# Feature order turned, edge columns with the folds, leads and delays per unit, load order and last store of an FNet-plus-FFN kernel

## The chip, the cores and the metric

The kernel runs on one core of a Trainium2 chip. The metric is the device time of one execution in microseconds; of several runs the median is taken. TensorE (PE) multiplies matrices and writes to PSUM. VectorE (DVE) and ScalarE (ACT) do arithmetic on SBUF and PSUM, GpSimd (POOL) on SBUF. SyncE (SP), ACT and POOL issue DMAs, each on a queue of its own. Every engine takes its instructions in the order in which they were written and waits on semaphores of the others.

## The reference

```python
def _attn_ref(x):                      # x: 8 x 3008 x 256
    X = np.fft.fft(x, axis=1)
    X = np.fft.fft(X, axis=2)
    return X.real.astype(np.float32)

def _moe_ref(x, w_in, w_out):          # 24064 x 256, 256 x 2048, 2048 x 256
    h = np.maximum(x @ w_in, 0.0)
    return (h * h @ w_out).astype(np.float32)
```

The real part of a two-dimensional Fourier transform of each of eight batches, and on its 24064 rows a feed-forward layer with squared relu.

## The kernel before, in words

**Folding.** The real part of the transform is symmetric, so a batch is handled by half of its rows and half of its columns. `fold_ops(b)` (L326) adds the two mirrored row halves of a batch on DVE (`u`, L334 and L338), makes their sums and differences (`v`, L346), and from each of these two features by adding or subtracting the mirrored columns (`w`, L352, 127 columns). Column 0 is copied to column 127 of `w` (L358) and column 128 to a separate tile of edges (`ez`, L360, for the first two batches, or `eall`, L362).

**Stage one.** `stage1_ops` (L409) multiplies the features by cosine and sine tables of the sequence transform (matmuls `pf`), ACT copies one parity from PSUM (`as`, L398), and DVE adds and subtracts the two parities into `pt` and `qt`, 1505 columns per batch (L427 to L434). The tables are made at the start by DVE (reduction of the angles, L237 to L249), ACT (sine) and mirror copies scaled by small vectors (`alt`, `nalt`, `sgn` and others, made by POOL, L168 to L182). The transform over the columns is folded into the input weights: `gmat` (L301) multiplies w_in by the matrices `csD` to G1 and G2, and `gneg` makes G3.

**Chunks and units.** The 12040 columns of `pt` and `qt` are cut into 25 chunks: two of 256, then 512, the last of 264. A chunk passes 16 units of 128 hidden features; a pair of such units is one step in the two short chunks, and one unit is a step in the others. A step has a front (first matmuls into PSUM tile `xb`) and, `LAG` = 2 steps later, a back (last matmuls into the same tile). Each unit gives the hidden values of a column and those of its mirror column. A letter in `KINDS` (L491) says how:

- r: three matmuls of the chunk's width, both relus on ACT (L607, L675).
- v: the same three, with the mirror's relu on DVE (L672).
- d: two matmuls. DVE makes an edge product X from `eb` and `gE2` (L634) and T = X − 2·xb (L653); ACT does the first relu (L663), DVE the mirror by a custom add with relu (L664).
- q: like d, but ACT copies −2·xb (L650) and POOL adds X (L651).
- p: like d, with X made by POOL (`edge`, L626). It is in the code, but no unit has it.

Pairs of units are squared by DVE (L687) or, where `SQA` (L492) lists them, by ACT in two halves (L684, L685). The second layer, `mm2_ops` (L513), then multiplies the squared values by w_out (matmuls `po`, 128x256), 16 per output tile; two output tiles share a PSUM tile, ACT copies it to SBUF (L558) and SP stores it in one or two DMAs per output tile (L547). The `po` matmuls of a chunk are spread over the steps of the next one.

**What sets the order.** The order is written out by hand: each step emits its front, half of its `po` matmuls, the back of two steps before, the other half, due mirrors (delay `DLAG`, L619, 1 step for all), copies of finished outputs, ACT's second square halves, the next unit's edge product, squares (3 steps after the back, 1 in the two short chunks), and side work: folds, stage one and tables of later batches, spread between fractions of a batch's time (`FOLD`, `ST1`).

**The start.** DMAs of x(0) go out on SP, POOL (gathers) and ACT (four small rows). ACT loads w_in in four quarters behind the second of eight mirror copies (L714). After the folds of batch 0 POOL loads w_out in four parts and then x(1) (L721). Ten warm matmuls on the cleared tile `ez` (L719) keep TensorE busy before the first real ones.

Of the kernel before, what the change touches and what calls it, by code (L numbers as in the profile page):

```python
# [18 lines left out]
HS = 32.0  # L19
# [5 lines left out]
def kernel(  # L25
# [103 lines left out]
    for s in range(2):  # L129
        gather(0, 1 - s)  # L130
        nc.sync.dma_start(out=x4[0:NP, s, :, :], in_=up(0, s))
    jm = h2p.tile([P, 3, P], F32, name="jm", tag="h2")
    jrow = jm[:, 0]
    nc.gpsimd.iota(jrow, pattern=[[1, P]], base=1, channel_multiplier=0,
# [33 lines left out]
    def alt_vecs():  # L168
        nc.gpsimd.tensor_scalar(out=alt, in0=pidx, scalar1=0.5, scalar2=-0.25, op0=ALU.mult, op1=ALU.add)
        nc.gpsimd.tensor_scalar(out=alt2, in0=alt, scalar1=R23, scalar2=None, op0=ALU.add)  # L170
        nc.gpsimd.tensor_scalar(out=alt2, in0=alt2, scalar1=R23, scalar2=None, op0=ALU.subtract)
        nc.gpsimd.tensor_tensor(alt, alt, alt2, op=ALU.subtract)
        nc.gpsimd.tensor_scalar(out=alt, in0=alt, scalar1=4.0, scalar2=None, op0=ALU.mult)
        nc.gpsimd.tensor_scalar(out=nalt, in0=alt, scalar1=-1.0, scalar2=None, op0=ALU.mult)
        nc.gpsimd.tensor_scalar(out=alt1, in0=top, scalar1=2.0, scalar2=alt[:, 0:1], op0=ALU.mult, op1=ALU.add)
        nc.gpsimd.tensor_scalar(out=nalt1, in0=alt1, scalar1=-1.0, scalar2=None, op0=ALU.mult)

    def sgn_vecs():
        nc.gpsimd.tensor_scalar(out=sgn, in0=pidx, scalar1=P - 1.5, scalar2=None, op0=ALU.is_lt)
        nc.gpsimd.tensor_scalar(out=s3, in0=sgn, scalar1=-2.0, scalar2=None, op0=ALU.mult)  # L180
        nc.gpsimd.tensor_scalar(out=sgn, in0=sgn, scalar1=2.0, scalar2=-1.0, op0=ALU.mult, op1=ALU.add)
        nc.gpsimd.tensor_scalar(out=nsgn, in0=sgn, scalar1=-1.0, scalar2=None, op0=ALU.mult)  # L182
# [9 lines left out]
    def dmats():  # L192
        pv = nc.gpsimd
# [6 lines left out]
        pv.memset(csD[:, 0, 0, P - 1 : P], 1.0)  # L200
        alt_vecs()
# [123 lines left out]

    def fold_ops(b):  # L326
        u = uvp.tile([P, 2, NQ, D], F16, name="u", tag="u")
        vs = {}
# [11 lines left out]
        def half(h, s):  # L340
            qs = slice(h * NQ // 2, (h + 1) * NQ // 2)

            def f():
                if h == 0:
                    vs[s] = uvp.tile([P, NQ, D], F16, name="v", tag="v")
                vt(vs[s][k, qs, :], u[k, 0, qs, :], u[k, 1, qs, :],  # L346
                   op=ALU.subtract if s else ALU.add)
            return f

        def feat(i, q):  # L350
            s = i % 2
            return lambda: vt(w[k, i, q : q + 3, 0 : P - 1], vs[s][k, q : q + 3, 1:P],  # L352
                              vs[s][k, q : q + 3, D - 1 : P : -1],
                              op=ALU.add if i < 2 else ALU.subtract)

        def edges(s):
            def f():
                nc.vector.tensor_copy(w[k, s, :, P - 1], vs[s][k, :, 0])  # L358
                if b in INL:
                    nc.vector.tensor_copy(ez[k, s, :, P - 1], vs[s][k, :, P])  # L360
                else:
                    nc.vector.tensor_copy(eall[k, s, :, b], vs[s][k, :, P])  # L362
            return f

        ops = [f for s in range(2) for f in (pair(s, 0), pair(s, 1), pair0(s))]
        if b + 1 < B:
            ops.append(lambda: load_x(b + 1))
        par = [[half(h, s) for h in range(2)] + [edges(s)]
               + [feat(i, q) for i in (s, 2 + s) for q in (0, 3)] for s in range(2)]
# [39 lines left out]
    def stage1_ops(b, blk, inline_e=False, run=3):  # L409
# [12 lines left out]
        def fin(sn):  # L422
            def f(a, bp):
                hi = P - 1 if sn and not inline_e else P
                lo_, hi_ = halves(blk, PQ[b][sn][0:hi])
                if sn and inline_e:
                    stt(out=lo_, in0=a, scalar=sgn[:, 0:1], in1=bp, op0=ALU.mult, op1=ALU.add)  # L427
                    stt(out=hi_, in0=bp, scalar=nsgn[:, 0:1], in1=a, op0=ALU.mult, op1=ALU.add)
                else:
                    vt(lo_, a, bp, op=ALU.add)  # L430
                    if sn:
                        vt(hi_, a, bp, op=ALU.subtract)
                    else:
                        vt(hi_, bp, a, op=ALU.subtract)  # L434
# [56 lines left out]
    KINDS = ["vrvrrrrrrrrrrrrr"] + ["rrrrvrrvrrrrrrrr"] + ["rvrrvvrrrvrrrrrr"] + ["rrrrrrrqdrrdrrrr"] + ["rdqqrrqrqrrrdrrq"] + ["rrrrddrrqrqrdqqq"] + ["rrrrrrqqqddrrdqd"] + ["rrdrqqdrrdrrqrqr"] + ["rqdddrqrrdrdrrdr"] + ["qddrqrdrrrdqddrr"] + ["drddqrdrrrddqrdr"] + ["qrrdrdddrrdrqrqr"] + ["drrdrqdrrddrdrqr"] + ["rrqdrdqrqqrrrddr"] + ["rrddqdqqrrqqdqqq"] + ["rrrrrrqqqddqrqrd"] + ["qdrdddrdqdrqdqrr"] + ["drdqqqrdqrqdrqqr"] + ["qdqqdqrqqrqdrqrq"] + ["dddrdqrdrqqdrqdq"] + ["dddrdqdrqrqdrddr"] + ["qdqqdqrdqrqdrqqr"] + ["qrqddqrqqrqdrqdr"] + ["qdqqdqvqqrqdqrdr"] + ["rddrdddddrdrdrdd"]  # L491
    SQA = [()] + [(3,)] + [(2, 6)] + [(0, 4, 5)] + [(0, 2, 5, 6)] + [(0, 4, 6)] + [(2, 3, 7)] + [(4, 6)] + [(5, 7)] + [(2, 5, 6)] + [(3, 7)] + [(0, 2, 6)] + [(0, 2, 5, 6)] + [(2, 4, 6)] + [(3,)] + [(1, 4, 6, 7)] + [(1, 2, 6)] + [(1, 4, 6)] * 2 + [(1, 4, 5, 6, 7)] + [(1, 4, 6)] * 3 + [(1, 4, 6, 7)] + [(0, 1, 6)]  # L492
# [20 lines left out]
    def mm2_ops(c):  # L513
# [36 lines left out]
        def store(grp, po):  # L550
# [157 lines left out]
    for h in range(2):  # L708
        for f in rd0[5 * h : 5 * h + 5] + (tr0[5:] if h else tr0[:5]):
            f()  # L710
# [163 lines left out]
```

## Time and profile before

| | |
|---|---|
| time, median of 9 runs | 604.55 us (603.03 to 605.39) |
| the profiled execution | 603.28 us |
| its span, first to last instruction | 601.5 us |
| PE busy | 581.4 us (97%) |
| ACT busy | 541.8 us (90%) |
| DVE busy | 526.7 us (88%) |
| POOL busy | 186.7 us (31%) |
| DMA | 56.25 MB, mean 94 GB/s |
| granted TensorE clock, mean | 0.999 |

Busy time counts stretches in which an instruction of the engine runs; ends of matmuls are modelled and overlap the next one, so the mean of one matmul (272 ns for 256 columns) is longer than the spacing of two. A row of a group has line, engine, operation, output and inputs, shape and count; then busy time and mean; then the idle time before, with what ended it. A row in order of time has start, length, engine, line and operation, with merged repeats as "x2".

### The profile page before, as it was taken

Reading aid. Unit: us, or ns where it says so; the run is one execution under the profiler, and the core shown is the slowest. Engines: PE = TensorE matmul, PEld = TensorE weight load, DVE = VectorE, ACT = ScalarE, POOL = GpSimd, SP = SyncE. Lnnn points to the kernel's source line nnn. Section 1 sums busy time; section 2 is a strip of 40 time slices with the busy share of each in tenths; the row PEclk is TensorE's granted clock in tenths of the full one; section 3 lists DMA queues with packets and bytes.
Section 4 is the critical chain, followed back from the end, with each engine's and each line's share of the span. In section 5 each row is a group of like instructions: output and inputs, shape, how many; then the busy total and the mean of one; then the engine's idle time right before and its main releaser. Section 6 shows DMA issues by size and latency. Waiting matters only on the chain.

```text
span 601.5 us, 12271 instructions
## 1 busy us (share of the span) xinstructions
PE 581.4 (97%) x4561; PEld 437.5 (73%) x4561; DVE 526.7 (88%) x954; ACT 541.8 (90%) x965; POOL 186.7 (31%) x177
## 2 busy tenths in 40 slices
PE   2899999999999999999999999999999999999997
PEld 0576676767777777777877778777787778877786
DVE  7899979998998999998889897989999989889880
ACT  5899899999998898889999989998998999999981
POOL 8502216412352014111113152322552323445300
PEclk9999999999999999999999999999999999999999
DMA  8967599673384225823133112331341422432212
GB/s 255 260 129 177 123 204 225 139 197 50 53 209 91 54 58 103 205 42 44 55 62 44 55 39 60 45 47 50 63 62 36 62 41 58 58 48 55 58 54 71
DMA packets 42337, 56.25 MB, mean 94 GB/s; under 512 B 8158, under 2 KB 37138, under 8 KB 42278
## 3 DMA queue, kind: packets, MB, share of 16 engines
q1 hardware_dynamic: 33878, 29.05, 25.8%
q0 software_dynamic: 7264, 24.31, 16.8%
q10 hardware_dynamic: 1136, 2.12, 1.1%
q8 instruction: 35, 0.57, 0.4%
q14 instruction: 24, 0.20, 0.1%
HBM read 29.02 MB, written 24.64 MB: 89 GB/s over the span
## 4 chain that ended last, share of the span: by engine, by line
PE 84%; ACT 9%; DVE 4%; POOL 1%; issue 1%; ACTq 0%; DVEq 0%; POOLq 0%
PE po L73 50%; PE xb L73 29%; PE pf L73 5%; ACT h L607 2%; ACT h L675 1%; ACT h L684 1%; ACT h L663 1%; ACT h L685 1%; DVE h L664 1%; DVE u L334 1%; POOL x L101 1%; ACT bs L650 0%; DVE v L346 0%; ACT os L558 0%; DVE bs L653 0%
## 5 line engine op out<-in xcount | busy, mean ns | idle before, releaser
L73 PE MATMUL po<-wout,h 128*128 128x256 f16 x3024 | 450.0, 272 | 0.0
L73 PEld LDWEIGHTS <-h 128*128 128x128 f16 x3024 | 286.3, 98 | 109.4 <-issue 0.6
L651 POOL TENSOR_TENSOR bs<-bs,h 128x512 f32<-128x512 f32 x99 | 133.7, 1353 | 311.4 <-ACT bs L650 213.2
L73 PE MATMUL xb<-qt,G 128*128 128x512 f16 (+11 forms) x758 | 211.3, 321 | 1.8 <-ACT h L607 0.9
L664 DVE CUSTOM_DVE_ANT_0 h<-xb,bs 128x512 f16<-128x512 f32 (+1 forms) x217 | 137.5, 642 | 24.2 <-ACT h L663 23.2
L687 DVE TENSOR_TENSOR h<-h 128x2048 f16<-128x2048 f16 (+1 forms) x122 | 149.6, 1229 | 0.4 <-ACT h L675 0.4
L73 PE MATMUL xb<-pt,G 128*128 128x512 f16 (+16 forms) x512 | 146.4, 323 | 1.0 <-DVE pt L434 0.5
L73 PEld LDWEIGHTS <-G 128*128 128x128 f16 x1270 | 121.3, 98 | 25.4 <-issue 4.4
L663 ACT ACTIVATE h<-xb 128x512 f16<-128x512 f32 (+1 forms) x206 | 129.1, 628 | 8.2 <-PE xb L73 6.4
L607 ACT ACTIVATE h<-xb 128x512 f16<-128x512 f32 (+1 forms) x178 | 110.6, 625 | 12.8 <-PE xb L73 12.4
L675 ACT ACTIVATE h<-xb 128x512 f16<-128x512 f32 (+2 forms) x174 | 105.3, 609 | 11.3 <-PE xb L73 9.2
L653 DVE SCALAR_TENSOR_TENSOR bs<-xb,h 128x512 f32<-128x512 f32 (+1 forms) x107 | 70.6, 660 | 17.3 <-PE xb L73 13.5
L634 DVE TENSOR_SCALAR h<-eb,gE 128x512 f16<-128x512 f16 (+1 forms) x206 | 79.6, 394 | 0.7 <-DMA eb<-qt 0.7
L685 ACT ACTIVATE h<-h 128x1024 f16<-128x1024 f16 (+1 forms) x70 | 74.9, 1070 | 0.0
L684 ACT ACTIVATE h<-h 128x1024 f16<-128x1024 f16 (+1 forms) x70 | 73.8, 1055 | 0.0
L558 ACT ACTIVATE os<-po 128x512 f32<-128x512 f32 x94 | 59.1, 629 | 8.7 <-PE po L73 8.6
L650 ACT ACTIVATE bs<-xb 128x512 f32<-128x512 f32 x99 | 63.5, 641 | 3.0 <-PE xb L73 1.4
L334 DVE TENSOR_TENSOR u<-x 127x765 f16<-127x765 f32 x32 | 30.6, 976 | 1.0 <-DMA x<-in_x_dram 1.0
L124 POOL DMA_DIRECT2D x<-in_x_dram x14 | 8.3, 593 | 58.8 <-DVE u L338 58.8
L73 PEld LDWEIGHTS <-w 127*128 127x128 f16 (+1 forms) x192 | 21.8, 117 | 5.6 <-DVE cosT L280 0.6
L101 POOL DMA_INDIRECT x<-in_x_dram,idx x18 | 23.4, 1298 | 5.4 <-issue 4.9
L352 DVE TENSOR_TENSOR w<-v 127x381 f16<-127x381 f16 x64 | 21.3, 357 | 0.0
(103 smaller groups left out, 227.4 us busy)
## 6 DMA issues: line engine op xcount, KB each, us to landing
out_dram<-os SPq DMA_DIRECT2D x157, 128.0 KB
x<-in_x_dram POOLq DMA_DIRECT2D x14, 756.0 KB, 10.9
wst<-in_moe_w_in_dram ACTq DMA_DIRECT2D x4, 512.0 KB
eb<-qt SPq DMA_DIRECT2D x14, 128.0 KB
x<-in_x_dram SPq DMA_DIRECT2D x2, 756.0 KB
wout<-in_moe_w_out_dram POOLq DMA_DIRECT2D x4, 256.0 KB, 7.0
x<-in_x_dram,idx POOLq DMA_INDIRECT x18, 11.2
gE<-G SPq DMA_DIRECT2D x16, 0.2 KB
```

Source lines behind the costliest of these rows:

```text
L73: nc.tensor.matmul(o, l, r, start=start, stop=stop, skip_group_check=True)
L607: act(r_s(c, u), xb, AF.Relu, scale=-1.0)
L634: ts(out=X, in0=ebc[c][:, 0:n], scalar1=gE2[:, u : u + 1], scalar2=None, op0=ALU.mult)
L650: act(T, xb, AF.Copy, bias=0.0, scale=-2.0)
L651: nc.gpsimd.tensor_tensor(T, T, X, op=ALU.add)
L653: stt(out=T, in0=xb, scalar=-2.0, in1=X, op0=ALU.mult, op1=ALU.add)
L663: act(r_s(c, u), xb, AF.Relu, scale=-1.0)
L664: mirrors.append((DLAG[KINDS[c][u]], lambda: relu_d(c, u, lambda o, i: nc.vector._custom_dve(TENSOR_ADD_SAT, out=o[:, 0, :], in0=xb[:, 0, ...
L675: relu_d(c, u, lambda o, i: act(o, xb[:, :, i], AF.Relu, scale=-1.0))
L684: act(h2[:, 0:nf], h2[:, 0:nf], AF.Square)
L685: rest.append(lambda: act(h2[:, nf:], h2[:, nf:], AF.Square))
L687: vt(h2, h2, h2, op=ALU.mult)
```

## The change

1. `KINDS` and `SQA` are rewritten: r 185 → 174, v 9 → 11, d 107 → 105, q 99 → 95, p 0 → 15; pairs squared by ACT 70 → 76.
2. Every d, q or p unit has its own lead for the edge product (`LEAD`, in half steps, 2 mostly) and its own delay of the mirror (`DEFER`, 1 mostly); every pair has its own lag of the square (`SQLAG`, 3 mostly; in chunk 0 the lags are 1, 1, 1, 2).
3. The features come in turned order, with 128 columns: `v` gets two zero columns, and column 0 is added to one of them by the same subtraction, so that the copy to column 127 of `w` is gone. `v` is a constant tile now.
4. At the start `alt_vecs`, `sgn_vecs` and the angles of `csD` go from POOL to DVE, the clear of `ez` from DVE to POOL behind the two gathers. 18 warm matmuls instead of 10. One more table operation stands before the second pair of folds.
5. The first quarter of w_in is issued by ACT behind the first mirror, the other three behind the sixth. POOL loads x(1) before w_out.
6. In stage one of batch 0 the second halves of `pt` and `qt` are put off behind both first halves. The stretches for folds and stage one of batches 0 to 2 are shifted a little.
7. In the last output group all 16 matmuls of the first tile come before those of the second, and each half is copied and stored by itself.

```diff
     for s in range(2):
         gather(0, 1 - s)
         nc.sync.dma_start(out=x4[0:NP, s, :, :], in_=up(0, s))
+    nc.gpsimd.memset(ez, 0.0)
...
-    nc.gpsimd.iota(jrow, pattern=[[1, P]], base=1, channel_multiplier=0,
+    nc.gpsimd.iota(jrow, pattern=[[-1, P]], base=P - 1, channel_multiplier=0,
...
-        nc.gpsimd.tensor_scalar(out=alt, in0=pidx, scalar1=0.5, scalar2=-0.25, op0=ALU.mult, op1=ALU.add)
...
+        ts(out=alt, in0=pidx, scalar1=0.5, scalar2=-0.25, op0=ALU.mult, op1=ALU.add)
...
-        pv = nc.gpsimd
+        pv = nc.vector
...
+    vf = const.tile([P, NQ, D + 2], F16, name="v")
+    nc.gpsimd.memset(vf[:, :, D : D + 2], 0.0)
...
-        def feat(i, q):
-            s = i % 2
-            return lambda: vt(w[k, i, q : q + 3, 0 : P - 1], vs[s][k, q : q + 3, 1:P],
-                              vs[s][k, q : q + 3, D - 1 : P : -1],
+        def feat(i, q, n):
+            return lambda: vt(w[k, i, q : q + n, :], vf[k, q : q + n, P - 1 :: -1],
+                              vf[k, q : q + n, P + 1 : D + 1],
                               op=ALU.add if i < 2 else ALU.subtract)
 
         def edges(s):
-            def f():
-                nc.vector.tensor_copy(w[k, s, :, P - 1], vs[s][k, :, 0])
...
+            e = ez[k, s, :, P - 1] if b in INL else eall[k, s, :, b]
+            return lambda: nc.vector.tensor_copy(e, vf[k, :, P])
...
-                    vt(hi_, bp, a, op=ALU.subtract)
+                        later(lambda: vt(hi_, bp, a, op=ALU.subtract))
...
-            act(os_, po, AF.Copy, bias=0.0, scale=HS * HS)
-            for j, (s, t0, m) in enumerate(grp):
+            js = js or slice(0, len(grp))
+            act(os_[:, js], po[:, js], AF.Copy, bias=0.0, scale=HS * HS)
+            for j, (s, t0, m) in list(enumerate(grp))[js]:
...
+                if fc == NFC - 1 and grp is final:
+                    return lambda o=st["o"]: store(grp, o, slice(j, j + 1))
...
+        final = groups[-1] if c == len(chunks) - 1 else None
         for grp in groups:
-            ops += [one(grp, j, fc) for fcs in (range(NFC - 2 * nf), range(NFC - 2 * nf, NFC))
+            cut = NFC if grp is final else NFC - 2 * nf
+            ops += [one(grp, j, fc) for fcs in (range(cut), range(cut, NFC))
                     for j in range(len(grp)) for fc in fcs]
...
-    DLAG = {'q': 1, 'd': 1, 'p': 1}
...
-    for f in rd1[0:2] + mi0[0:2] + [load_w_in] + mi0[2:] + fe[0:3] + rd1[2:3]:
+    for f in rd1[0:2] + mi0[0:1] + [lambda: load_w_in(0)] + mi0[1:6] + [lambda: load_w_in(1, 2, 3)] + mi0[6:] + fe[0:3] + rd1[2:4]:
         f()
...
-    for _ in range(10):
+    for _ in range(18):
         mm(warm, ez[:, 0, 0, :], ez[:, 0, 0:4, :], True, True)
-    for f in fe[3:6] + [load_w_out] + fe[6:]:
+    for f in fe[3:]:
         f()
+    load_w_out()
...
-    spread(rd1[3:], 0, 5)
-    spread(fo, 8, 9)
+    spread(rd1[4:], 0, 5)
+    spread(fo, 7, 13)
...
-    FOLD = {0: [(1, 0.489, 0.896)], 1: [(2, 0.02, 0.073), (3, 0.261, 0.695), (4, 0.581, 0.851)],
+    FOLD = {0: [(1, 0.467, 0.852)], 1: [(2, 0.068, 0.189), (3, 0.261, 0.695), (4, 0.581, 0.851)],
...
-    ST1 = {0: (0.9, 0.945)}
+    ST1 = {0: (0.855, 0.885)}
...
+    for si, (c, u) in enumerate(steps):
+        if KINDS[c][u] in "qdp":
+            l = int(LEAD[c][u])
+            ahead.setdefault((si - l // 2, l % 2), []).append((c, u))
...
+            if v[1] % 2:
+                squares.setdefault(si + int(SQLAG[v[0]][v[1] // 2]), []).append(v)
```

## The prediction

> **What bounds the kernel now.** I read the page's busy shares first, then the chain that ended last, then the costliest groups.
>
> ```profile
> PE 581.4 (97%) x4561; PEld 437.5 (73%) x4561; DVE 526.7 (88%) x954; ACT 541.8 (90%) x965; POOL 186.7 (31%) x177
> ...
> PE 84%; ACT 9%; DVE 4%; POOL 1%; issue 1%; ACTq 0%; DVEq 0%; POOLq 0%
> ...
> L73 PE MATMUL po<-wout,h 128*128 128x256 f16 x3024 | 450.0, 272 | 0.0
> ```
>
> TensorE is the bound: 97% busy, and 84% of the chain. But ScalarE and VectorE stand at about 90%, so a small local excess on either one shows. Next, the stretches in which TensorE was not full (columns: stretch, its length, PE, PEld, DVE, ACT, POOL busy, clock, DMA share, GB/s):
>
> ```profile
> 22.80:33.00 10.20, 9.72 (x76) 7.16 (x74) 9.52 (x18) 10.15 (x21) 1.66 (x3) 1.00 1.16 237
> ...
> 71.00:77.00 6.00, 5.65 (x50) 3.59 (x49) 5.86 (x18) 5.98 (x11) 4.73 (x6) 1.00 0.77 202
> 88.00:103.00 15.00, 14.79 (x114) 10.60 (x113) 13.86 (x25) 14.93 (x27) 9.38 (x9) 1.00 0.91 200
> 120.00:123.00 3.00, 2.47 (x18) 1.74 (x17) 3.00 (x8) 3.00 (x6) 0.86 (x1) 1.00 0.99 253
> 490.00:496.00 6.00, 5.76 (x43) 4.01 (x42) 4.40 (x9) 6.00 (x12) 2.19 (x2) 1.00 0.39 54
> ```
>
> In each of them ACT is full, and at 120 DVE too. Everywhere else after 38.5 us TensorE runs without gaps. Busy ends are modelled, so I count starts instead: start-to-start times beyond the usual spacing add up to about 2.7 us in the last four stretches. That is all that can be won in the middle. Last, the start and the end, from the order of time:
>
> ```profile
> 5.48 0.25 POOL L318 MEMSET eall<- 128x161 f16 x1
> ...
> 11.24 0.68 DVE L237 TENSOR_TENSOR tm<-nval,krow 128x564 f32<-128x564 f32 x1
> ...
> 11.38 4.45 PE L73 MATMUL warm<-ez 128*128 128x512 f16 x10 [11.38 <-DVE ez L713]
> ...
> 17.41 0.59 PE L73 MATMUL pc<-win,csD 128*128 128x512 f16 x2 [1.57 <-ACT win L299]
> ...
> 17.91 1.16 DVE L352 TENSOR_TENSOR w<-v 127x381 f16<-127x381 f16 x4
> ...
> 18.48 1.13 PE L73 MATMUL pf<-cosT,w 127*128 127x377 f16 x6
> ```
> ```profile
> 597.29 0.60 ACT L558 ACTIVATE os<-po 128x512 f32<-128x512 f32 x1 [2.90 <-PE po L73]
> 597.92 0.81 SPq L547 DMA_DIRECT2D out_dram<-os  x2
> ```
>
> Stage one (pf) begins half a microsecond after VectorE's first features; after the last matmul come one copy, two store issues, the landing and the closing barrier.
>
> The profiled execution took 603.28 us (span 601.5, 1.8 around it). The median shown is 604.55, 1.27 above. I add the sum of changes to the median.
>
> **1. Fewer three-matmul units.** A unit of kind r or v streams three 512-column matmuls, one of kind d, q or p two. Counting the letters, r+v falls from 194 to 185: seven 512-column matmuls and two of 264 go. The chain shows two 512-column matmuls in 0.43 us, so 7 × 0.215 + 2 × 0.11 = **−1.73 us**. TensorE is the bound, so it counts nearly in full; it is worth nothing only where ACT is full.
>
> **2. Load moved to the others.** From the letters and the list of ScalarE squares, with the chain's pieces (ACT 0.49 per 512-wide, 0.94 per 1024-wide; DVE 0.60, 0.33, 1.13): ScalarE loses 11 r (−10.8), 4 q (−3.9) and 2 d (−1.0) and gains 15 p (+7.4), 2 v (+1.0) and six squared pairs (+11.3): +4 us in all. VectorE gains 15 p (+18.0) and 2 v (+1.2) and loses 2 d (−3.1), 4 q (−3.7), six squares (−6.8) and the edge copies (about −2): also +4. POOL gains 15 edges and loses 4 sums. By chunk: chunks 3 and 4, from about 70 to 118 us, lose 0.5 and 1.0 us of ACT; chunk 18, near 430 us, gains 1.4. I take 0.9 of the 1.5 us lost there as won, since ACT is what is full there: **−0.9**. The ends are −2.7 (all those stalls go) and +1.4 (chunk 18 stalls instead and nothing is won).
>
> The new leads, delays, square lags and places of folds and stage one change no amount of work. Their cover is the two steps (about 1.4 us each) between a unit's first matmul and its last, and six PSUM buffers; without it they are inside the ends of this term.
>
> **3. The start.** Before stage one VectorE gains eight alt vectors and four sign vectors (12 × 0.18, the spacing of its tiny dependent rows), four jm operations (4 × 0.25, the row of that shape) and one table operation (0.74), together 3.9. It loses the 0.7 us clear of ez and two waits for POOL (1.10 and 1.16) and one edge copy (0.1): 3.1. Stage one starts **+0.8** later. From 22.8 to 33 the chain is ACT in pieces of 0.49: one ScalarE mirror becomes kind v, −0.49. And the first square lag puts the first output matmul one step later; until then a step costs ACT 0.98 and TensorE only 0.66: +0.32. Together **+0.6**, ends −0.2 and +1.5. ScalarE's own start is not later: its table mirrors no longer wait for POOL and for four load issues in a row (1.02 and 1.78 idle), which more than pays for matrices that come 1 us later, so pc may start near 16.3. On ACT's queue the four weight loads (0.6 to 0.7 us of issue each) move: the first stands behind one mirror instead of two, the other three behind six. I cost that at nothing, since the quarters are copied only from 16.3 on, the next from 19.0; without that cover a copy waits, and pc with it, but stage one is later still. The two sums that are now put off (pt and qt, second halves) give nothing: qt's first half started at 21.66, when stage one's last matmul was done.
>
> The ten warm matmuls took 0.43 each, half rate, and those at 17.41 run at 0.215, after a gap of 1.6. Now 18 follow POOL's clear of ez (0.25 for 161 columns, 0.10 for one: about 1.5 for 1536, after the gathers end at 5.2), so from about 6.8 to 12.8, and the gap to pc is 3.5 or more. The two ends are this gap of 1.6, after which the clock was whole, and the 11.4 idle at the start, after which it was half. At half the 18 pf matmuls (0.16 each) take up to 2.9 more. I take 0, since the gap is nearer to 1.6.
>
> [...]
>
> **4. The output weights go behind the next x.** The transfers of window 24 to 40 (40 slices of 0.4 us, busy tenths):
>
> ```profile
> DMA  9999899899989999999999979989996696765121
> ```
>
> They are saturated until 39 us. Before, w_out was issued at 15.7 on POOL's queue, landed by 25, and x(1) came after it. Now x(1)'s six issues (about 6 us of POOL) are ahead of w_out's four (3.2 us), the same bytes move, and w_out's four quarters are the last 5.7 us (19 to 24.7 before): landing at 34 to 39. The first output matmul was at 32.97, now about 34. All later matmuls queue behind it. Ends: 0 and +2.9 (second and third quarter two to three us late). I take **+0.6**, near the low end, since x(1) may start 8 us sooner and the matmuls that need the last quarter come four steps later.
>
> **5. Features and edges.** Same number of subtractions, 384 columns for 381 (0.36 us each); the 0.25 us w copies go. The new v has one buffer as before. Nothing.
>
> **6. Last store in halves.** The last group now does all 16 matmuls of half 0, then half 1. In the built order half 1's first matmul waits for ScalarE's copy of half 0: 0.36 from the last start to the copy, 0.40 for it (a 16x256 copy took 0.37), less the 0.11 spacing: +0.7. After the end, a shorter copy (−0.2) and one issue and 128 KB less (−0.5). **0**, ends ±0.3.
>
> Sum: −1.73 − 0.9 + 0.6 + 0.6 + 0 = −1.4; 604.55 − 1.4 = **603.1**.
>
> **Rivals.**
> - *All stalls go, w_out is in time.* For it: ACT falls in the very chunks that stall. Against: chunk 18. −1.73 − 2.7 + 0.6 = −3.8: 600.7.
> - *w_out becomes the new wait.* For it: the saturated row. Price 2.9 in place of 0.6: 605.4.
> - *POOL's edges make it slower.* A p unit's 128x512 edge on POOL has no row. The nearest are 0.46 (two-input 128x128) and 1.02 × 4 = 4.1 (the slowest 128x128 tensor_scalar scaled to 512). Ten of the 15 have a lead of one step; with the two steps to the unit's last matmul that leaves 4.2, less 0.7 for VectorE's sum, 3.5 us. Above 3.5 TensorE waits at each; at 3.1 (the middle row, 0.78, × 4) only where a 1.16 us q sum or another p is ahead, some four times 0.8 = 3.2: **606.3**, slower.
> - *The clock falls back* for half of stage one: half of 2.9, +1.5, 604.6.
>
> [...]
>
> **How the numbers follow.** 0.2%, 1.2 us, is about what a measurement tells from none: faster is under 603.3, slower over 605.8. Forecast 0.38, own range 601.8 to 604.2 (0.24 faster, 0.14 same); stalls gone 0.24 (faster); w_out 0.18 (0.09 same, 0.09 slower); POOL 0.14 (slower); clock 0.06 (0.01 faster, 0.05 same). Faster 0.49, same 0.28, slower 0.23. The range goes from 600.4 to 606.3: it leaves out the better part of the second case (0.10) and the worse half of POOL's (0.07).
>
> **What would show it.** Step 1: 11 fewer xb matmuls. Step 2: the stretches at 71 to 103 with PE full; ACT full around 430 to 470. Step 3: pf's first start near 19.3, pc near 16.5 at 0.215 spacing (0.43 would be the clock). Step 4: TensorE waiting for wout's DMA near 34 us. Step 6: a gap of 0.7 us 16 matmuls before the end. Rival POOL: L653's counterpart waiting for POOL. I am wrong if stalls of more than 2 us appear after 123 us, where the trace of before has almost none.

## The result and the profile after

The changed kernel takes 608.73 us (median of 10 executions, 606.17 to 610.98). The kernel before took 604.55 us in the same comparison (31 executions, 602.65 to 605.39). The ratio is 1.0070, with a 95% interval of 1.0056 to 1.0083: 4.2 us slower. The forecast was 603.1 us, and its range ended at 606.3.

The profiled execution took 609.38 us, its span 607.5 us; before it was 603.28 and 601.5. So the profile has 6.1 us to explain. First the page of the changed kernel: busy shares, the granted clock in 40 slices, and the chain that ended last.

```profile
PE 586.2 (96%) x4558; PEld 439.3 (72%) x4558; DVE 522.0 (86%) x967; ACT 545.5 (90%) x961; POOL 179.2 (29%) x174
...
PEclk9799999999999999999999999999899999999999
...
PE 87%; DMA 6%; ACT 3%; DVE 2%; issue 1%; SPq 0%; POOL 0%; ACTq 0%; DVEq 0%; POOLq 0%
PE po L73 51%; PE xb L73 30%; PE pf L73 6%; DMA wout<-in_moe_w_out_dram 3%; DMA x<-in_x_dram 2%; DMA eb<-qt 1%; ACT h L667 1%; ACT os L559 1%; DMA out_dram<-os 0%; ACT h L688 0%; ACT bs L654 0%; ACT h L612 0%; ACT h L689 0%; DVE tm L237 0%; ACT h L679 0%
```

Two things are new. DMA has 6% of the chain: w_out 3%, x 2%, and the spread edge row `eb` 1%. And the clock has dips, in the second slice and in slice 29, near 430 us. TensorE is busy 4.8 us longer with three matmuls fewer, which points to the clock.

The same kind of table by stretches as was shown of before (stretch, its length, PE, PEld, DVE, ACT, POOL busy, clock, DMA share, GB/s):

```profile
22.80:33.00 10.20, 9.36 (x60) 6.29 (x59) 6.98 (x15) 7.32 (x15) 1.49 (x2) 0.89 1.08 188
71.00:77.00 6.00, 6.00 (x50) 3.98 (x49) 5.61 (x8) 6.00 (x13) 1.47 (x2) 1.00 0.25 63
88.00:103.00 15.00, 15.00 (x123) 10.80 (x122) 12.71 (x24) 14.57 (x26) 8.23 (x8) 1.00 0.84 213
120.00:123.00 3.00, 3.00 (x22) 1.99 (x21) 3.00 (x7) 3.00 (x6) 2.69 (x5) 1.00 0.91 237
430.00:440.00 10.00, 7.83 (x52) 5.56 (x51) 7.39 (x12) 6.54 (x11) 2.99 (x4) 0.83 0.22 56
```

The three old stalls from 71 to 123 us are gone: TensorE is full there. But at 430 us, where the kernel before had none, TensorE loses 2.17 us and the clock stands at 0.83. The start has grown too: 60 matmuls between 22.8 and 33 us, where there were 76.

**The stall at 430 us**, in order of time (start, length, engine, line, operation, and in brackets the idle time before it and what ended it):

```profile
425.19 1.12 SPq L621 DMA_DIRECT2D eb<-qt  x2
...
431.44 0.60 PE L73 MATMUL po<-wout,h 128*128 128x256 f16 x4
...
432.07 0.35 DVE L638 TENSOR_SCALAR h<-eb,gE 128x512 f16<-128x512 f16 x1 [4.04 <-DMA eb<-qt]
432.34 1.22 DVE L691 TENSOR_TENSOR h<-h 128x2048 f16<-128x2048 f16 x1
433.48 0.68 DVE L668 CUSTOM_DVE_ANT_0 h<-xb,bs 128x512 f16<-128x512 f32 x1
...
434.21 0.38 PE L73 MATMUL xb<-pt,G 128*128 128x326 f16 x2 [2.17 <-DVE h L668]
434.43 0.90 PE L73 MATMUL po<-wout,h 128*128 128x256 f16 x4
```

Read it from the bottom. TensorE waited 2.17 us for VectorE's mirror (L668), which frees a PSUM tile. That mirror stood behind the edge product at 432.07, and this one had waited 4.04 us for a DMA. SP had sent the edge row of chunk 18 in two parts at 425.19 and 425.72; by the chain of the trace the second was there at 431.97, 6.3 us after its issue. The product is that of chunk 18, unit 0, to which `LEAD` gives "8": four steps ahead. The row itself is sent six steps ahead (`si - 6`), so the product came up in VectorE's queue two steps, about 2.8 us, behind the issue of its own input. VectorE takes its instructions in order: no row of it starts in these 4.04 us, so everything behind the product waited as well. After that the matmuls are at half rate (four of 256 columns in 0.90 and then 1.06 us instead of 0.60).

**The start**, TensorE alone:

```profile
6.62 6.37 PE L73 MATMUL warm<-ez 128*128 128x512 f16 x18 [6.62 <-POOL ez L132]
16.46 0.59 PE L73 MATMUL pc<-win,csD 128*128 128x512 f16 x2 [3.48 <-ACT win L299]
...
19.09 2.07 PE L73 MATMUL pf<-cosT,w 127*128 127x377 f16 x6 [1.38 <-DVE w L349]
...
24.73 0.40 PE L73 MATMUL xb<-pt,G 128*128 128x256 f16 x1
```

Stage one begins at 19.09 (18.48 before), but its 18 matmuls take until 24.73, 5.64 us instead of 2.89 (18.48 to 21.37): they run at half clock, the granted clock being 0.50 from 18.2 to 24.9 us. After the 18 warm matmuls TensorE had stood idle for 3.48 us.

**The output weights**, POOL alone, and then TensorE alone where it first needs them:

```profile
14.61 0.60 POOL L124 DMA_DIRECT2D x<-in_x_dram  x1 [7.51 <-DVE u L341]
...
21.05 1.61 POOL L707 DMA_DIRECT2D wout<-in_moe_w_out_dram  x2
24.58 0.75 POOL L707 DMA_DIRECT2D wout<-in_moe_w_out_dram  x1 [1.92 <-DMA x<-in_x_dram]
28.65 0.74 POOL L707 DMA_DIRECT2D wout<-in_moe_w_out_dram  x1 [3.32 <-DMA x<-in_x_dram,idx]
```
```profile
38.59 0.60 PE L73 MATMUL po<-wout,h 128*128 128x256 f16 x4 [1.07 <-DMA wout<-in_moe_w_out_dram]
...
39.85 0.60 PE L73 MATMUL po<-wout,h 128*128 128x256 f16 x4 [0.45 <-DMA wout<-in_moe_w_out_dram]
```

The four parts are issued at 21 to 28.7 us (15.7 to 18.2 before); before the last two POOL waited 1.92 and 3.32 us, each time until a transfer of x had ended. Their median from issue to landing is 17.0 us, 7.0 before. TensorE's starts are 2.3 us beyond their usual spacing at 37 to 41 us.

**The end:**

```profile
601.64 0.38 ACT L559 ACTIVATE os<-po 128x256 f32<-128x256 f32 x1 [1.15 <-PE po L73]
602.07 1.91 PE L73 MATMUL po<-wout,h 128*128 128x256 f16 x16 [0.52 <-ACT os L559]
604.07 0.38 ACT L559 ACTIVATE os<-po 128x256 f32<-128x256 f32 x1 [2.04 <-PE po L73]
```

The second half waits for the copy of the first; from start to start that is 0.69 us beyond the spacing. From the last copy's start to the end of the span it is 3.5 us, 4.2 before.

To add this up I count TensorE's starts beyond the spacing that their columns take (0.11 us for 256, 0.22 for 512), the changed kernel less the kernel before. So the 6.1 us of the profile are, to 0.1: 4.0 us around 432 us (2.3 in the gap, 1.7 at half clock), 2.75 for stage one at half clock, 0.6 for its later start, 1.6 from 36 to 42 us (waits of 2.3 us for w_out, where the kernel before had 1.0 us of other gaps), 0.4 in small gaps near 500 us; less 1.73 us of columns and 1.6 us of old stalls (1.74 before, 0.14 now). The gap and the shorter copy at the end cancel. The experiments have to say which of these the time depends on, since what is lost early can be time that would have been lost later anyway.

### The profile page after: what moved, and what is told of

Its sections match the earlier page's. It is cut to its first block, busy times and chain, and to the rows that moved or that the text cites. A ratio compares the mean times of both kernels' runs of the same rounds, so it can differ in the third digit from the quotient of the medians.

```text
span 607.5 us, 12279 instructions
## 1 busy us (share of the span) xinstructions
PE 586.2 (96%) x4558; PEld 439.3 (72%) x4558; DVE 522.0 (86%) x967; ACT 545.5 (90%) x961; POOL 179.2 (29%) x174
## 4 chain that ended last, share of the span: by engine, by line
PE 87%; DMA 6%; ACT 3%; DVE 2%; issue 1%; SPq 0%; POOL 0%; ACTq 0%; DVEq 0%; POOLq 0%
PE po L73 51%; PE xb L73 30%; PE pf L73 6%; DMA wout<-in_moe_w_out_dram 3%; DMA x<-in_x_dram 2%; DMA eb<-qt 1%; ACT h L667 1%; ACT os L559 1%; DMA out_dram<-os 0%; ACT h L688 0%; ACT bs L654 0%; ACT h L612 0%; ACT h L689 0%; DVE tm L237 0%; ACT h L679 0%
## 5 line engine op out<-in xcount | busy, mean ns | idle before, releaser
L655 POOL TENSOR_TENSOR bs<-bs,h 128x512 f32<-128x512 f32 x95 | 122.8, 1295 | 310.6 <-ACT bs L654 255.6
L668 DVE CUSTOM_DVE_ANT_0 h<-xb,bs 128x512 f16<-128x512 f32 (+1 forms) x228 | 142.3, 637 | 23.1 <-ACT h L667 22.3
L691 DVE TENSOR_TENSOR h<-h 128x2048 f16<-128x2048 f16 (+1 forms) x116 | 141.0, 1218 | 0.5 <-ACT h L679 0.4
L612 ACT ACTIVATE h<-xb 128x512 f16<-128x512 f32 (+1 forms) x169 | 106.9, 636 | 12.0 <-PE xb L73 11.5
L679 ACT ACTIVATE h<-xb 128x512 f16<-128x512 f32 (+2 forms) x161 | 100.6, 629 | 9.8 <-PE xb L73 8.3
L657 DVE SCALAR_TENSOR_TENSOR bs<-xb,h 128x512 f32<-128x512 f32 (+1 forms) x120 | 78.8, 658 | 17.2 <-PE xb L73 13.7
L689 ACT ACTIVATE h<-h 128x1024 f16<-128x1024 f16 (+1 forms) x76 | 81.6, 1074 | 0.0
L688 ACT ACTIVATE h<-h 128x1024 f16<-128x1024 f16 (+1 forms) x76 | 80.7, 1062 | 0.1
L638 DVE TENSOR_SCALAR h<-eb,gE 128x512 f16<-128x512 f16 (+1 forms) x200 | 69.1, 360 | 7.6 <-DMA eb<-qt 7.6
L559 ACT ACTIVATE os<-po 128x512 f32<-128x512 f32 (+1 forms) x95 | 59.6, 627 | 9.2 <-PE po L73 9.2
L654 ACT ACTIVATE bs<-xb 128x512 f32<-128x512 f32 x95 | 59.6, 628 | 4.5 <-PE xb L73 3.1
L349 DVE TENSOR_TENSOR w<-v 127x384 f16<-127x384 f16 x64 | 23.6, 388 | 0.0
## 6 DMA issues: line engine op xcount, KB each, us to landing
x<-in_x_dram,idx POOLq DMA_INDIRECT x18, 10.7
```

The costliest lines, as they stand in the source:

```text
L559: act(os_[:, js], po[:, js], AF.Copy, bias=0.0, scale=HS * HS)
L612: act(r_s(c, u), xb, AF.Relu, scale=-1.0)
L638: ts(out=X, in0=ebc[c][:, 0:n], scalar1=gE2[:, u : u + 1], scalar2=None, op0=ALU.mult)
L655: nc.gpsimd.tensor_tensor(T, T, X, op=ALU.add)
L657: stt(out=T, in0=xb, scalar=-2.0, in1=X, op0=ALU.mult, op1=ALU.add)
L668: mirrors.append((int(DEFER[c][u]), lambda: relu_d(c, u, lambda o, i: nc.vector._custom_dve(TENSOR_ADD_SAT, out=o[:, 0, :], in0=xb[:, 0, i ...
```

## The experiments

Each kernel was timed in five rounds beside the kernel before. That kernel's own medians were 604.75, 603.82 and 604.38 us in the three groups below, so across groups ratios are compared, and a difference under 0.15% is not resolved.

### First group: one suspect at a time

**w_out back at its old place in the program** (ahead of x(1)):

```diff
-    for f in fe[3:]:
+    for f in fe[3:6] + [load_w_out] + fe[6:]:
         f()
-    load_w_out()
```

> Only the loads of w_out go back to where they stood before the change, ahead of the second batch's x. Theory W (the late w_out costs what the three gaps of TensorE at 37 to 41 us show, 1.23 + 0.61 + 0.49 us over the usual spacing): the three waits 'PE po <- DMA wout' are gone, 2.3 us less than the changed kernel, ratio to the kernel before near 1.003. The rest (matmuls of the first stage at half clock, the stall at 432 us) stands as it was. Rival L (the gaps at 37 to 41 us only take the place of waits for the second batch's features, which x behind w_out would make late): the waits turn into waits for x or for pt and qt of the second batch, and the time stays within 0.5 us of the changed kernel, ratio 1.006 to 1.008.

Measured: 617.89 us, ratio 1.0228 (1.0204 to 1.0252). Both theories fail. The profile, POOL alone and then the longest waits of VectorE:

```profile
6.99 0.11 POOL L201 MEMSET csD<- 128x1 f16 x1
7.03 3.14 POOL L707 DMA_DIRECT2D wout<-in_moe_w_out_dram  x4
15.45 0.58 POOL L124 DMA_DIRECT2D x<-in_x_dram  x1 [5.28 <-DVE u L341]
```
```profile
DVE win L299 <- DMA wst<-in_moe_w_in_dram: 11.5, 2, 6.4
```

The old place in the program is not the old time. Before the change POOL had twelve small vectors and the angles of `csD` to compute, and this held its w_out loads back until 15.7 us, behind the w_in loads at 10.7 to 12.4. The change gave that work to VectorE. POOL is free at 7.0 us, w_out goes first, and w_in, issued at 11.4 to 12.9, arrives late: VectorE's two casts wait 11.5 us for it, ACT's 2.6. So the two moves of the change belong together: with POOL emptied, w_out has to go behind something.

**More warm matmuls:**

```diff
-    for _ in range(18):
+    for _ in range(34):
```

> 34 warm matmuls in place of 18, so that TensorE has work from 6.6 us up to the first product with w_in near 16.5 us; nothing else. Theory C (the granted clock fell at 18.15 us because TensorE stood idle from 12.8 to 16.46 us): the clock stays full from 11.3 us on, the 18 matmuls of the first transform take 2.9 us again instead of 5.64. But w_out still lands at 36 to 40 us, so the 2.75 us come back as a longer wait for it: the waits for w_out grow from 2.3 to about 4 to 5 us, and the time falls by only 0.3 to 1 us (ratio 1.005 to 1.0065). Rival D (the matmuls wait for their features, not for the clock): they take as long as before and no time moves, ratio 1.007. Rival I (both costs are independent): the whole 2.75 us are gained, ratio 1.0025.

Measured: 608.71 us, ratio 1.0066 (1.0041 to 1.0090): no time moved. Yet the clock did what theory C says. TensorE alone:

```profile
19.09 1.14 PE L73 MATMUL pf<-cosT,w 127*128 127x377 f16 x6 [0.60 <-DVE ez L355]
...
21.99 0.27 PE L73 MATMUL xb<-pt,G 128*128 128x256 f16 x1
...
37.99 0.60 PE L73 MATMUL po<-wout,h 128*128 128x256 f16 x4 [1.84 <-DMA wout<-in_moe_w_out_dram]
```

The 18 matmuls take 2.90 us again and stage one ends 2.74 us earlier. TensorE then waits for w_out, which starts the first `po` at 37.99, only 0.60 us earlier than in the changed kernel. Rival D gives the right time for the wrong reason: the half clock is real, and it is covered by the later w_out. Where two losses lie one behind the other at the same gate, removing the first one shows nothing.

**The one lead:**

```diff
-    LEAD = [...] + ["8222222222222222"] + [...]
+    LEAD = [...] + ["2222222222222222"] + [...]
```

> The lead of the edge product of unit 0 of chunk 18 goes from 8 to 2, so that it is put into VectorE's queue one step ahead of its unit instead of four; nothing else. Theory E (VectorE works in order, the product waits 4.04 us for the spread edge row that was sent for only two steps earlier, and what stands behind it starves TensorE; the gap then lets the clock fall for one window of 3.4 us): no gap near 432 us, no half clock at 434.6 us, 3.9 us less than the changed kernel, ratio near 1.0005. Rival N (the wait falls upon slack of VectorE that is needed a step later anyway): the gap moves to a neighbouring step, 0 to 1 us less. Rival K (the clock falls there without the gap): only the 2.3 us of the gap are gained, ratio 1.003.

Measured: 604.59 us, ratio 1.0003 (0.9985 to 1.0022): 4.1 us less than the changed kernel, by changing one character of the source. The same stretch:

```profile
425.00:435.00 10.00, 10.00 (x82) 7.71 (x80) 8.82 (x17) 9.72 (x18) 5.06 (x4) 1.00 0.41 55
```

TensorE is full, the clock is 1.00. Theory E stands, and both rivals fall. This is as large as the whole loss against the kernel before, with an interval of about 1 us to either side. Sending the row earlier, with the lead left at 8, was not tried.

**All three together:**

> The three edits together: w_out ahead of the second batch's x, 34 warm matmuls, the lead of unit 0 of chunk 18 at 2. If the three places are the whole of the loss, the gains add to 2.3 + 2.75 + 3.9 = 8.9 us: 599.8 us, ratio near 0.992, and the clock is full from 11.3 us to the end. If the new assignment of units to engines itself is the loss (VectorE's queue, GpSimd's edge products), what is left is above the kernel before, ratio 1.001 to 1.004, with the waits spread over 120 to 600 us.

Measured: 615.20 us, ratio 1.0182 (1.0158 to 1.0207). The early w_out spoils it as in the first run; casts wait 12.7 us for w_in. It tells only that the other two edits are worth 2.7 us beside that loss.

### Second group: w_out at its old time, the old start, the last stores

**w_out between the halves of x(1)**, with the lead mended:

```diff
     def load_x(b):
         for s in range(2):
             nc.gpsimd.dma_start(out=x4[0:NP, s, :, :], in_=up(b, s))
             gather(b, 1 - s)
+            if b == 1 and s == 0:
+                load_w_out()
...
-    load_w_out()
```

> Lead of chunk 18's first edge product at 2 as in the run before, and the loads of w_out are put into GpSimd's queue between the two halves of the second batch's x: behind the first half's wait for VectorE, so near 17 us, where the kernel before issued them (15.7 to 18.2 us), and not at 7 us. Theory W2 (w_out is late because it stands behind all of x(1), whose second half is issued at 17.7 to 20.5 us; and issued at 7 us it takes the bandwidth of w_in): no wait 'PE po <- DMA wout', no wait for w_in beyond the 0.7 to 2.6 us that are there, 1.5 to 2.5 us less than with the lead alone (604.6): 602.1 to 603.1, ratio 0.9955 to 0.9975. Rival S (any w_out ahead of the rest of w_in and x slows what the start waits for): the casts of w_in wait over 3 us and the time is at least that with the lead alone, ratio 1.000 or more.

Measured: 603.85 us, ratio 0.9987 (0.9973 to 1.0002); with the lead alone it was 1.0003. The loads are issued at 17.3 to 19.6 us, land in 11.9 us, and no wait for w_out is left; the casts of w_in wait 0.8 us. Theory W2 holds in its waits. Its gain is 1.0 us (1.0003 to 0.9987), less than the 1.5 to 2.5 expected, and the two intervals overlap.

**The same with 34 warm matmuls:**

> The same with 34 warm matmuls. Theory C2 (34 warm matmuls kept the clock full in their run, and the time stood still only since w_out ended the wait at 40 us anyway): with w_out there in time the faster first stage counts: clock full from about 11 us to the end, 1.5 to 2.75 us less than the same without them: about 600.3 us, ratio 0.991 to 0.995. Rival G (the start is then bound by the casts of w_in on VectorE and ACT, not by TensorE): 0 to 0.7 us less.

Measured: 603.39 us, ratio 0.9979 (0.9964 to 0.9994), 0.5 us less. In the profiles the difference is what theory C2 says; TensorE alone, first without and then with the longer warm-up:

```profile
19.08 2.07 PE L73 MATMUL pf<-cosT,w 127*128 127x377 f16 x6 [1.18 <-DVE w L351]
...
24.64 0.27 PE L73 MATMUL xb<-pt,G 128*128 128x256 f16 x1
```
```profile
19.07 1.14 PE L73 MATMUL pf<-cosT,w 127*128 127x377 f16 x6 [1.03 <-DVE w L351]
...
21.96 0.27 PE L73 MATMUL xb<-pt,G 128*128 128x256 f16 x1
```

That is 2.7 us in these two executions (604.68 and 602.20 us), but over twelve executions the medians differ by 0.5 us, within rival G's 0 to 0.7. Part of it is that the clock's loss varies: without the longer warm-up the mean granted clock was 0.997 in five of the twelve executions and 0.993 to 0.996 in the others, and the former took 603.0 us on average, the latter 604.1; with it the clock was 0.999 or 1.000 in all, and the mean 603.1. What sets the rest of the spread was not found.

**The start of the kernel before** under the new interior:

```diff
-        pv = nc.vector
+        pv = nc.gpsimd
...
-    nc.gpsimd.memset(ez, 0.0)
+    nc.vector.memset(ez, 0.0)
...
-    for f in rd1[0:2] + mi0[0:1] + [lambda: load_w_in(0)] + mi0[1:6] + [lambda: load_w_in(1, 2, 3)] + mi0[6:] + fe[0:3] + rd1[2:4]:
+    for f in rd1[0:2] + mi0[0:2] + [load_w_in] + mi0[2:] + fe[0:3] + rd1[2:3]:
...
-    for _ in range(18):
+    for _ in range(10):
...
-    for f in fe[3:]:
+    for f in fe[3:6] + [load_w_out] + fe[6:]:
         f()
-    load_w_out()
...
-    s1 = stage1_ops(0, 0, True, 1, hi_ops)
+    s1 = stage1_ops(0, 0, True, 1)
```

(`alt_vecs` and `sgn_vecs` go back to POOL too.)

> The start of the kernel before (the small vectors and the angles of the 128-point tables on GpSimd, w_in in one piece, w_out at its old place, 10 warm matmuls, the mirrored rows of the first stage at once) under the changed kernel's feature order, assignment, leads, delays and last stores; the lead of chunk 18's first product at 2. Theory A (the loss sits in the start and in the one lead; the new assignment is a gain): from the kernel before, less 1.73 us of columns and about 2 us of stalls at 71 to 123 us that are gone in the changed kernel's trace: 600.8 us, ratio 0.992 to 0.9955. Rival B (the new assignment gains only what its own new waits give back): ratio 0.997 to 1.000.

Measured: 602.55 us, ratio 0.9975 (0.9959 to 0.9990): faster than the kernel before, and inside rival B's range; theory A's range is missed. The profile shows two things that stood in the way of theory A. One is the clock. TensorE alone:

```profile
17.56 1.01 PE L73 MATMUL pc<-win,csD 128*128 128x512 f16 x2 [1.71 <-ACT win L299]
```

Two `pc` matmuls take 1.01 us, where they took 0.59 before: they still run at half clock, though the ten warm matmuls were the same. The first six `pf`, at 19.64 us, take 1.58 us (1.13 before), the next three, at 21.07, 0.65 as before, and stage one ended at 22.99 us (21.37 before). The mean granted clock of this execution reads 1.000 all the same. It does not show what is lost here: in the kernel before, too, the stretch of the ten warm matmuls (11.4 to 15.8 us) reads 1.00, though they take 0.43 us each. In four of the twelve executions the mean reads 0.997. The other thing is a new gap, all engines in order of time:

```profile
37.97 0.55 ACT L261 ACTIVATE cosT<-tt,hpl 128x188 f16<-128x188 f32 x1
...
38.88 0.86 ACT L261 ACTIVATE cosT<-tt,hpl 128x564 f16<-128x564 f32 x1
...
39.54 0.69 ACT L612 ACTIVATE h<-xb 128x512 f16<-128x512 f32 x1
...
40.28 0.38 PE L73 MATMUL xb<-qt,G 128*128 128x256 f16 x2 [1.05 <-ACT h L612]
```

Seven sine activations of the second table block stand on ACT in one row, two of the last three here, and the relu behind them (L612) frees the PSUM tile that TensorE wants. The change puts the last two of them into the step of the other five, `spread(tr1[5:], 11, 12)`; with the `11, 13` of the kernel before, the seventh came a step later, behind two relus. In the changed kernel this gap is inside the wait for w_out.

**The last stores as before**, on the run with 34 warm matmuls:

```diff
-                if fc == NFC - 1 and grp is final:
-                    return lambda o=st["o"]: store(grp, o, slice(j, j + 1))
...
-            cut = NFC if grp is final else NFC - 2 * nf
+            cut = NFC - 2 * nf
```

> As the run with w_out between the halves of x(1) and 34 warm matmuls, but the last group is computed and stored as in the kernel before, both tiles together. By the profile the halves put one wait of 0.5 us (gap 0.69 us) on TensorE near the end and shorten the last eviction from 0.63 to 0.38 us: undoing them takes the gap away and lengthens the end by 0.25 to 0.6 us. Expected against the same run with halves: between 0.4 us less and 0.2 us more, ratio within 0.001; the gap near 595 us is gone. Rival (halves hide a whole eviction and transfer): 0.6 to 1 us more.

Measured: 603.22 us, ratio 0.9985 (0.9968 to 1.0001), against 603.39 and 0.9979 with halves: no difference that can be told. In the profiles the gap is gone, and from the start of the last copy to the end of the span it is 4.2 us instead of 3.5: the 0.7 us of the gap against 0.7 us at the end.

### Third group: the rest of the gap, and what the interior is worth

**The sine activations over two steps**, on the run with 34 warm matmuls:

```diff
-    spread(tr1[5:], 11, 12)
+    spread(tr1[5:], 11, 13)
```

> As the run with w_out between the halves of x(1), 34 warm matmuls and the lead at 2, but the last seven Sin activations of the second table block are spread over two steps as in the kernel before, not put into one. In the profile of that run seven of them stand in a row on ACT (35.5 to 38.5 us) and the Relu behind them makes TensorE wait 1.0 us at 37.94 us, where the kernel before had a gap of 0.5 us. Theory T: the gap shrinks from 1.2 to about 0.5 us, 0.7 us less, about 602.7 us, ratio near 0.997. Rival: the wait passes to the block's matmuls (they need the last table) and nothing is gained.

Measured: 602.63 us, ratio 0.9975 (0.9960 to 0.9989), 0.2 us less by the ratios (0.9979). The gap before the relu's tile shrank from 1.20 to 0.55 us, and two of 0.17 and 0.20 came at the block's own matmuls, as the rival says in part. In time the two runs are not told apart.

**The old start with both edits** (16 warm matmuls instead of 10, and the line above):

> As the run with the start of the kernel before, with 16 warm matmuls in place of 10 and the Sin activations spread over two steps as in the kernel before. Three executions of that run had the clock at half for a window and took 603.5 to 604.0 us, those with full clock 601.3 to 602.7. Theory C2 and T together: clock full in all, no 1.2 us gap at 38.9 us: 601.0 to 601.8 us, ratio 0.994 to 0.9965. Rival: the start is bound by the features, so that only the gap counts: 602, ratio 0.997.

Measured: 601.60 us (600.88 to 602.50), ratio 0.9963 (0.9952 to 0.9975). This is the fastest kernel of the study, 0.37% under the kernel before and 1.1% under the changed one. The mean granted clock reads 1.000 in all eleven executions; in this trace the first two `pc` take 0.59 us, the full rate. The start is that of the kernel before, 0.3 us later:

```profile
11.41 6.46 PE L73 MATMUL warm<-ez 128*128 128x512 f16 x16 [11.41 <-DVE ez L718]
17.70 0.59 PE L73 MATMUL pc<-win,csD 128*128 128x512 f16 x2
...
18.78 1.13 PE L73 MATMUL pf<-cosT,w 127*128 127x377 f16 x6
```

**The old assignment on this base** (`KINDS` and `SQA` of the kernel before; all leads 2, delays 1, lags 3 after chunk 1):

```diff
-    KINDS = [... of the changed kernel ...]
-    SQA = [... of the changed kernel ...]
+    KINDS = [... of the kernel before ...]
+    SQA = [... of the kernel before ...]
-    LEAD = [...]
-    DEFER = [...]
-    SQLAG = [...]
+    LEAD = ["2" * 16] * 25
+    DEFER = ["1" * 16] * 25
+    SQLAG = ["1112", "3133"] + ["3" * 8] * 23
```

> As the run with the old start, 16 warm matmuls and spread Sin activations, but with the kernel before's assignment of units to engines and of squares to ACT, and all leads, delays and lags uniform as there. Against that run it measures what the new assignment with its lists is worth in the interior. By the trace: 8 columns-worth of three-matmul units back, 1.73 us, and the stalls of TensorE at 71 to 123 us back, 2.2 us, less the gaps of 0.36 and 0.48 us at 499 and 506 us: 3 us more, 604 to 604.8, ratio 0.999 to 1.001. Rival (the stalls left when the features were computed in another order, not through the assignment): 1.2 to 1.7 us more.

Measured: 604.05 us, ratio 1.0002 (0.9991 to 1.0014), 2.4 us more than the base. The size is near the first forecast, the reason is not. The stretches of this run:

```profile
43.00:57.00 14.00, 12.86 (x91) 8.59 (x89) 13.92 (x27) 10.66 (x19) 5.51 (x6) 1.00 0.61 155
71.00:77.00 6.00, 6.00 (x53) 4.05 (x52) 5.93 (x11) 6.00 (x12) 2.83 (x4) 1.00 0.44 110
88.00:103.00 15.00, 15.00 (x122) 10.88 (x121) 13.80 (x23) 14.63 (x28) 7.74 (x8) 1.00 0.89 176
120.00:123.00 3.00, 3.00 (x24) 2.21 (x23) 3.00 (x8) 3.00 (x6) 2.48 (x4) 1.00 1.01 263
```

The stalls from 71 to 123 us do not come back with the old assignment. So it was not the assignment that took them away, and the rival is right in this point. What is back is 11 matmuls (4567 for 4556), 1.73 us, and new waits, by starts 1.6 us between 43 and 57 us (1.1 us of it idle in the row) and 0.5 us at 38 us. Against them stand 0.7 us at 90 us and 0.4 us near 495 us that only the base loses. What makes the new waits was not followed; the kernel before, with the same assignment, has none between 43 and 57 us.

**The lists alone** (new assignment; `LEAD`, `DEFER` and `SQLAG` as in the last diff):

> The same base with the new assignment kept, and only leads, delays and lags uniform (2, 1, 3). My prediction costed these lists at nothing. If so, within 0.5 us of the base, 601 to 602. Rival U (the lists stagger work that otherwise collides on VectorE): stalls appear in the chunks whose lists differ, 1 us more or over. Rival H (the leads of 4 to 8 put products ahead of their spread edge rows): the waits for the edge rows, 3 us in sum, go, and the time falls by up to 0.5 us.

Measured: 602.99 us, ratio 0.9982 (0.9971 to 0.9992), 1.1 us more than the base by the ratios, 1.4 by the medians. Rival U holds: gaps of 0.76 us at 401, 1.36 from 479 to 485 and 0.20 at 583 us come up, and gaps of 0.83 at 491 and 498 and 0.46 at 90 us shrink or go. The waits for edge rows fall from 3.0 to 0.4 us, as rival H says, but the time does not fall with them.

## Why the prediction was wrong, step by step

**Step 1, fewer three-matmul units, −1.73: right.** The `xb` matmuls on `qt` fall from 758 to 747, their columns are the 1.73 us, and on a common base the new assignment with its lists is worth 2.4 us, of which 1.1 to 1.4 are the lists.

**Step 2, load moved, −0.9 with ends −2.7 and +1.4: this is the step that failed, and in its last sentence.** It said that leads, delays and lags "change no amount of work", that "their cover is the two steps (about 1.4 us each) between a unit's first matmul and its last, and six PSUM buffers", and costed them at nothing. One of the leads cost 4.1 us. The cover that was named is that of a product that comes too late. A lead of 8 makes it come too early: it is put into an in-order queue ahead of its input, a DMA that took 6.3 us here, and then it holds up what others need now. The two numbers to compare were in the code, a product four steps ahead and a row six steps ahead, with 1.4 us a step; the kernel before had its products one step ahead, five steps behind the row, so its profile showed waits of 0.4 us at most. The place was named (chunk 18, near 430 us), but for another reason, ACT's 1.4 us. The prediction's own test, "stalls of more than 2 us appear after 123 us", is what happened.

The stalls from 71 to 123 us did go: 1.74 us by starts before, 0.14 us in the changed kernel, more than the 0.9 taken. (The forecast had 2.7 us for the last four stretches; counted so, they are 2.3.) But not for ACT's lighter load in chunks 3 and 4: from 71 to 77 us ACT is as full as before, 6.00 of 6.00 us, and with the old assignment the stalls are gone as well. Nor are they gone for good, since the base of the third group, with the new assignment, has 0.74 us at 90 us. Which of the remaining edits did it (feature order, edge copies or the folds' places) was not settled. Of the two loads forecast at +4 us, ACT's came out at +3.7 us of busy time; VectorE's fell by 4.7 us instead, its edge products alone by 10.5 us (79.6 to 69.1).

**Step 3, the start, +0.6, and the clock at 0.** Stage one began at 19.09 (forecast near 19.3), `pc` at 16.46 (16.3 to 16.5). The gap of 3.5 us was foreseen to the tenth, and the wrong end was taken for it. The row it leaned on, a gap of 1.6 us with a whole clock behind it, was no evidence: there the ten warm matmuls ahead of the gap took 0.43 us each and the two `pc` behind it 0.59 us together, so the clock was not kept through the gap but came up in it. In the changed kernel the clock did fall, to 0.50 from 18.2 to 24.9 us, and in the profile stage one took 2.75 us longer, near the upper end of 2.9. In time, though, the term is small: 0 as long as w_out is the gate, about 0.5 us when it isn't, and that 0.5 is not clear of the noise. The Sin activations that the change puts into one step were left out of the sum; they make the relu late by 1.05 us where w_out does not hide it.

**Step 4, w_out, +0.6 with ends 0 and +2.9.** Waits came where they were forecast, but later: the four parts landed at 38.6 to 42.5 us, where 34 to 39 was forecast, and the first output matmul came at 38.6, not 34. In the profile they are 2.3 us, by the runs 1.0 us. The rival that put 2.9 here had the profile nearly right.

**Step 5, features and edges, nothing:** no run measured it by itself.

**Step 6, the last stores, 0: right,** with its parts: the gap was forecast at 0.7 and is 0.7, the shorter end at −0.7 and is −0.7.

**POOL's edge products:** the rival falls. They take 0.70 us in the median (15 of them, 11 of 512 and 4 of 264 columns), TensorE never waits for one, and VectorE once, 0.6 us. (Eleven of them, not ten, have a lead of one step.)

In sum, by the runs: with the old start (and its clock kept whole) and the lead mended, the new interior is 2.2 us under the kernel before by the ratio, 2.8 by the medians. The new start costs 2.4 to 3.0 us against that (from 0.9963 to 1.0003; 601.60 to 604.59), where steps 3 and 4 had +1.2. The one lead costs 4.1. That makes −2.5 + 2.7 + 4.1 = +4.3 us, and +4.2 was measured; as the three steps run from one measured kernel to the next, the sum has to come out and is no further test. The forecast of −1.4 had the first term, half of the second, and none of the third. That the first agrees (−1.73 − 0.9 = −2.6) is partly luck: 0.9 of it was expected from ACT's lighter load, which the runs do not bear out. And between the two profiled executions the gain is 1.7 us of span only (601.5 to 599.8), so a part of the 2.2 to 2.8 us may be the steadier start, whose times spread from 600.9 to 602.5 us against 602.7 to 605.9; this was not separated.

## What to carry to other kernels

Before an operation is moved ahead in an in-order queue, find the issue of its inputs and the time that this transfer takes in the trace, and check that the operation still stands behind the landing: a wait that comes too early stops work that has nothing to do with it (here VectorE started nothing for 4.04 us). An instruction's place in the program is not its time: what leaves an engine's queue lets all that stood behind it start earlier, DMA issues too (10 us of small work taken off POOL let the same load start at 7.0 us instead of 15.7, ahead of a more urgent one). When a cause is taken away and no time moves, look for the next wait on the same path before the cause is dismissed; here the clock and the late weights lay one behind the other.

## What the runs showed of the hardware

**The clock at half.** In the changed kernel's trace the clock stands at half in two stretches while TensorE has work: from 18.15 to 24.98 us, 6.83 us long, and from 434.58 to 437.99 us, 3.41 us long. By stretches, TensorE alone (stretch, length, busy time, clock, DMA share, GB/s):

```profile
11.40:14.70 3.30, 1.59 (x8) 1.00 0.91 297
14.80:18.10 3.30, 1.24 (x5) 1.00 1.01 362
18.20:24.90 6.70, 5.81 (x19) 0.50 1.06 241
...
431.20:434.50 3.30, 1.13 (x10) 1.00 0.19 63
434.60:437.90 3.30, 3.30 (x16) 0.50 0.00 0
```

TensorE is idle for part of each of the three rows at 1.00, and what follows them differs: behind 1.24 of 3.30 us busy, and behind 1.13 of 3.30, the clock is at half; behind 1.59 of 3.30 it is whole. In the two rows at 0.50 TensorE is busy for 5.81 of 6.70 us and for 3.30 of 3.30. These are single stretches of one trace; what the clock goes by they do not show.

At the start, the ten warm matmuls were followed by two `pc` in 0.59 us in the kernel before and in 1.01 us under its start in the second group; sixteen, 6.46 us long, were followed by two in 0.59 us. Why the same ten are followed by the full rate once and by half of it once is not shown.

A gap of nearly the same length went without the loss in another run. With w_out at its old place in the program the gap at the same lead is 2.04 us of idle time (2.17 in the changed kernel), and the clock is whole on both sides of it:

```profile
438.00:441.40 3.40, 2.20 (x17) 1.00 0.43 89
441.50:444.80 3.30, 2.57 (x22) 1.00 0.00 0
```

So the gap of 2.17 us was followed by 1.7 us lost at half clock, and the one of 2.04 us by no such loss. What decides between the two is not shown. The executions of the changed kernel spread from 606.2 to 611.0 us, at mean clocks of 0.991 to 0.997; those of the kernel whose mean clock always read 1.000 spread from 600.9 to 602.5 us. The first run with 34 warm matmuls, which kept the long lead, points the same way: two executions with a mean clock of 1.000 took 606.8 and 608.7 us, four with 0.997 took 608.3 to 610.4. That the clock is what makes the spread is argued, not shown, for only one execution of each kernel has a trace.
